# A decode-attention block: eight heads of one batch row at a time, V in 64-KB rows, TensorE in a loop, each engine written by itself

## The chip, the core and the metric

The kernel runs on one core of one Trainium2 chip. The metric is the device time of one execution in microseconds. The kernel before was run three times: the median is 668.3 us, the lowest 667.74 and the highest 669.08.

## What is computed

One decode step of a transformer block for four sequences (B = 4) with one new token each. Everything is bf16 at the boundary.

```python
# x (4,1,640); k_cache, v_cache (4,32,4096,128); wq (640,4096); wo (4096,640); w1 (640,1728); w2 (1728,640)
q = (layernorm(x) @ wq).reshape(4, 1, 32, 128).transpose(0, 2, 1, 3)
p = softmax(einsum("bhqd,bhkd->bhqk", q, k_cache) * 128**-0.5)
o = einsum("bhqk,bhkd->bhqd", p, v_cache)
h = x + o.transpose(0, 2, 1, 3).reshape(4, 1, 4096) @ wo
u = layernorm(h) @ w1 + b1
out = h + (u * tanh(softplus(u))) @ w2
```

The two caches hold 134.2 MB each; wq and wo 5.2 MB each; w1 and w2 2.2 MB each. Every byte of them is read once.

## The kernel before

The attention is done in 32 groups (`NG`). A group is four neighbouring heads of one batch row. Its keys are one tile of 4 MB in SBUF: 128 partitions, 32 of them for each head, and 128 consecutive keys in each partition, which are 32 KB in a row both in memory and in SBUF (L100). The values lie the same way in a second tile. There are two buffers for K tiles and two for V tiles (`KBUFS`, `VBUFS`).

A group's work runs through all engines.

- VectorE multiplies the K tile in place by the query, in four pieces of 4096 elements per partition (L367). The query has been spread over the partitions beforehand (`qbs`).
- TensorE adds each piece up over the 128 columns by multiplying with the identity (L374), eight matmuls of 512 columns to a piece, and VectorE reduces what is left in PSUM to 64 scores per partition (L386), twice to a group.
- The softmax takes the maximum of a partition (L397), brings it to one row by TensorE (L399), takes the maximum of each head (L404), sends it back to the partitions (L412), and ScalarE makes the exponentials (L417), which also writes them spread into the four columns of a head selector `e2`.
- TensorE multiplies V by them (L257, 32 matmuls of 512 columns to a group), ScalarE copies the result out of PSUM (L267), and TensorE adds the blocks up (L273).

The order is written out by hand in one Python loop over the groups, with the framework's schedule switched off; the framework still places the waits and the semaphores. All large loads are issued by SyncE's queue (SP): wq first, then two K tiles and a V tile, and then each next tile as its buffer comes free. The output projection's weights wo come in between groups 8 and 11 in eight loads (L471), and the weights of the MLP, w1 and w2, are the last loads (L502 to L508). Of the last group, K is loaded in two parts and V in four.

At the end stand the last group's softmax, the last projection (L348), the second layernorm, the two MLP products (L564, L629) and a 5-KB store (L653).

Of the kernel before, what the change touches and what calls it, by code (L numbers as in the profile page):

```python
# [12 lines left out]
AX = mybir.AxisListType  # L13


@with_exitstack
def kernel(
# [23 lines left out]

    nc = tc.nc

# [4 lines left out]
    DC = D // 128  # L48
    G = 4
    PH = 128 // G  # L50
    R = Sk // PH
    NP = 2
    RP = R // NP
    W = 512 // RP
    HQ = H // G
    NG = HQ * N
    SCALE = float(Dh) ** -0.5
    EPS = 1e-5
    QC = 512
    WOC = 8  # L60
    NQ = 2
    DQ = Dh // NQ
    VP = 4
    KBUFS = 2
    VBUFS = 2
    NE2 = 2

# [5 lines left out]
    FC = C2 + 1  # L73

    W1_PARTS = ((0, 3), (3, DC))

    ctx.enter_context(tc.manual_schedule())


    pad = ctx.enter_context(tc.tile_pool(name="pad", bufs=1))  # L80
    pad.tile([128, 192], BF16, name="pad")
    kpool = ctx.enter_context(tc.tile_pool(name="kpool", bufs=KBUFS))
    vpool = ctx.enter_context(tc.tile_pool(name="vpool", bufs=VBUFS))
    wbig = ctx.enter_context(tc.tile_pool(name="wbig", bufs=1))
    consts = ctx.enter_context(tc.tile_pool(name="consts", bufs=1))
    work = ctx.enter_context(tc.tile_pool(name="work", bufs=2))

    x_rows = A_x.rearrange("b s d -> (b s) d")
    out_rows = out.rearrange("b s (c p) -> (b s c) p", p=128)


    def load_kv(pool, tag, cache, g, parts):
        hq, b = divmod(g, N)
        t = pool.tile([128, R, Dh], BF16, tag=tag, name=f"{tag}{g}")
        view = cache[b, G * hq : G * (hq + 1)].rearrange("h (p r) d -> (h p) r d", p=PH)

        np_ = parts if g == NG - 1 else 1
        for i in range(np_):
            r0, r1 = i * R // np_, (i + 1) * R // np_
            nc.sync.dma_start(out=t[:, r0:r1, :], in_=view[:, r0:r1, :])  # L100
        return t

    def load_k(g):
        return load_kv(kpool, "kt", A_k_cache, g, NP)

    def load_v(g):
        return load_kv(vpool, "vt", A_v_cache, g, VP)

    x_bf = consts.tile([N, D], BF16)
    nc.scalar.dma_start(out=x_bf[:, :], in_=x_rows[:, :])  # L110

    wq_sb = wbig.tile([128, DC, H * Dh], BF16, tag="w")
    nc.sync.dma_start(out=wq_sb[:, :, :], in_=A_wq.rearrange("(p c) n -> p c n", c=DC))
    kts, vts = {}, {}
    kts[0] = load_k(0)
    kts[1] = load_k(1)
    vts[0] = load_v(0)


    ident = consts.tile([128, 128], BF16)  # L120
    make_identity(nc, ident[:, :])
    ident_f = consts.tile([128, 128], FP32)
    nc.gpsimd.tensor_copy(out=ident_f[:, :], in_=ident[:, :])
    ones_f = consts.tile([128, 128], FP32)
    nc.gpsimd.memset(ones_f[:, :], 1.0)
    mean_f = consts.tile([128, 128], FP32)
    nc.gpsimd.memset(mean_f[:, :], 1.0 / D)
    eps_t = consts.tile([128, 1], FP32)
    nc.vector.memset(eps_t[:, :], EPS)
    nscale = consts.tile([1, 128], FP32)  # L130
    nc.vector.memset(nscale[:, :], -SCALE)
    sel = consts.tile([N, N, G, 128], BF16)
    nc.vector.memset(sel[:, :, :, :], 0.0)
    e2 = [consts.tile([128, R, G], BF16, name=f"e2_{i}") for i in range(NE2)]
    for t in e2:
        nc.gpsimd.memset(t[:, :, :], 0.0)
    rs2 = consts.tile([128, NG, G], FP32)
    nc.gpsimd.memset(rs2[:, :, :], 0.0)
    b1T = consts.tile([128, FC], FP32)
    nc.gpsimd.memset(b1T[:, :], 0.0)  # L140
    otn = consts.tile([128, HQ, N, G], BF16)

    for q in range(G):
        nc.vector.tensor_copy(
            out=sel[:, :, q, q * PH : (q + 1) * PH],
            in_=ident[0:N, 0:N].unsqueeze(2).to_broadcast([N, N, PH]),
        )

    def layernorm_rows(in_sb, out_bf, pool):
        n_sub = 2  # L150
        in_view = in_sb.rearrange("p (n f) -> p n f", n=n_sub)
        stats = pool.tile([N, n_sub, nc.vector.BN_STATS_DIM], FP32, tag="ln_stats")
        for s in range(n_sub):
            nc.vector.bn_stats(out=stats[:, s, :], in_=in_view[:, s, :])
        mv = pool.tile([N, nc.vector.BN_AGGR_DIM], FP32, tag="ln_mv")
        nc.vector.bn_aggr(out=mv[:, :], in_=stats[:, :, :])
        std = pool.tile([N, 1], FP32, tag="ln_std")
        nc.scalar.activation(
            out=std[:, :], in_=mv[:, 1:2], func=ACT.Sqrt, bias=eps_t[0:N, :], scale=1.0
        )  # L160
        rstd = pool.tile([N, 1], FP32, tag="ln_rstd")
        nc.vector.reciprocal(out=rstd[:, :], in_=std[:, :])
        nc.vector.tensor_scalar(
            out=out_bf[:, :],
            in0=in_sb[:, :],
            scalar1=mv[:, 0:1],
            scalar2=rstd[:, :],
            op0=ALU.subtract,
            op1=ALU.mult,
        )  # L170


    ps_cm = tc.tile_pool(name="ps", bufs=1, space=bass.MemoryType.PSUM)
    ps = ps_cm.__enter__()

    ln1_bf = consts.tile([N, D], BF16)
    layernorm_rows(x_bf, ln1_bf, work)
    xT = consts.tile([128, DC, N], BF16)
    xT_res = consts.tile([128, DC, N], FP32)
    ln1_v = ln1_bf[:, :].rearrange("n (p c) -> n c p", c=DC)  # L180
    x_v = x_bf[:, :].rearrange("n (c p) -> n c p", c=DC)
    for src, dst in ((ln1_v, xT), (x_v, xT_res)):
        tp_ps = ps.tile([128, DC, N], FP32, tag="small")
        for c in range(DC):
            nc.tensor.matmul(
                tp_ps[:, c, :], lhsT=src[:, c, :], rhs=ident[0:N, 0:N], start=True, stop=True
            )
        nc.vector.tensor_copy(out=dst[:, :, :], in_=tp_ps[:, :, :])

    q_all = consts.tile([N, H * Dh], BF16)  # L190

    def q_chunk(n):
        q_ps = ps.tile([N, QC], FP32, tag="qq")
        for c in range(DC):
            nc.tensor.matmul(  # L195
                q_ps[:, :],
                lhsT=xT[:, c, :],
                rhs=wq_sb[:, c, n * QC : (n + 1) * QC],
                start=(c == 0),
                stop=(c == DC - 1),  # L200
            )
        nc.scalar.copy(out=q_all[:, n * QC : (n + 1) * QC], in_=q_ps[:, :])  # L202

    def q_broadcast(hq):
        qb_ps = ps.tile([128, N * Dh], FP32, tag="qq")
        for b in range(N):
            for q in range(G):
                h = G * hq + q
                nc.tensor.matmul(  # L209
                    qb_ps[:, b * Dh : (b + 1) * Dh],  # L210
                    lhsT=sel[:, b, q, :],
                    rhs=q_all[:, h * Dh : (h + 1) * Dh],
                    start=(q == 0),
                    stop=(q == G - 1),
                )
        nc.scalar.copy(
            out=qbs[:, hq, :, :], in_=qb_ps[:, :].rearrange("p (b d) -> p b d", d=Dh)
        )

    qbs = consts.tile([128, HQ, N, Dh], BF16)  # L220

    Q_AT = {-1: (0,), **{g: (g + 1,) for g in range(HQ - 1)}}
    WO_AT = {HQ + i: i for i in range(H // WOC)}
    B1_AT = HQ + len(WO_AT) + 1

    PROJ_AT = {B1_AT + 1 + hq: hq for hq in range(4)}
    PROJ_AT.update({4 * (hq + 1) + 2: hq for hq in range(4, HQ - 1)})
    for hq in Q_AT[-1]:
        q_chunk(hq)
        q_broadcast(hq)  # L230

    ot = {}


    J = 4
    T = 4
    p_ps = ps.tile([128, J * Dh], FP32, tag="p")
    nc.vector.memset(p_ps[:, :], 0.0)
    pick = consts.tile([128, J * G], FP32)
    nc.vector.tensor_reduce(  # L240
        out=pick[:, :],
        in_=ident_f[:, :].rearrange("p (t i) -> p i t", t=T)[:, 0 : J * G, :],
        axis=AX.X,
        op=ALU.add,
    )
    blocks = {}

    def ot_of(g):
        hq, b = divmod(g, N)
        if b == 0:  # L250
            ot[hq] = ps.tile([128, N, G], FP32, tag="ot", name=f"ot{hq}")
        return ot[hq][:, b, :]

    def pv_moving(g, r0, r1):
        for r in range(r0, r1, J):
            c0 = 128 // T * (r // J % T)
            nc.tensor.matmul(  # L257
                p_ps[c0 : c0 + J * G, :],
# [6 lines left out]
    def pv_copy(g):  # L265
        blocks[g] = work.tile([128, J * Dh], FP32, tag="p_sb", bufs=1, name=f"p_sb{g}")
        nc.scalar.copy(out=blocks[g][:, :], in_=p_ps[:, :])  # L267
# [159 lines left out]
    for g in range(NG):  # L427
# [28 lines left out]
        if g in PROJ_AT:  # L456
            project(PROJ_AT[g])
# [227 lines left out]
```

## Time and profile before

| | |
|---|---|
| median of three runs | 668.3 us |
| the profiled execution, its own time | 667.85 us |
| its span, first to last instruction | 666.0 us |
| bytes read from HBM | 283.35 MB |
| DMA packets | 13,015 |
| instructions in the trace | 7,152 |
| TensorE busy, mean clock granted | 441.4 us (66%), 0.847 |
| VectorE busy | 353.0 us (53%) |
| ScalarE busy | 115.0 us (17%) |
| wq landed, first K tile landed | 15.95 us, 25.64 us |

The profile shows one execution. Its span leaves out 1.85 us of its own time. An engine's busy time is the time in which it worked on instructions; waits, branches and the issuing of DMAs are not in it. The DMA figures are a mean over the core's 16 DMA engines. The trace also holds a record of every DMA packet, with its start, its length in ns and its bytes.

### The profile page before, as it was taken

Reading aid. Unit: us, or ns where it says so; the run is one execution under the profiler, and the core shown is the slowest. Engines: PE = TensorE matmul, PEld = TensorE weight load, DVE = VectorE, ACT = ScalarE, POOL = GpSimd, SP = SyncE. Lnnn points to the kernel's source line nnn. Section 1 sums busy time; section 2 is a strip of 40 time slices with the busy share of each in tenths; the row PEclk is TensorE's granted clock in tenths of the full one; section 3 lists DMA queues with packets and bytes.
Section 4 is the critical chain, followed back from the end, with each engine's and each line's share of the span. In section 5 each row is a group of like instructions: output and inputs, shape, how many; then the busy total and the mean of one; then the engine's idle time right before and its main releaser. Section 6 shows DMA issues by size and latency. Waiting matters only on the chain.

```text
span 666.0 us, 7152 instructions
## 1 busy us (share of the span) xinstructions
PE 441.4 (66%) x3105; PEld 203.4 (31%) x3105; DVE 353.0 (53%) x308; ACT 115.0 (17%) x352; POOL 2.4 (0%) x13
## 2 busy tenths in 40 slices
PE   0588777886666475367666857766557785667786
PEld 0233333343223232133222323322223232223345
DVE  2486454466645266246654545657444666455742
ACT  0022122131101111011111111111011111011131
POOL 1000000000000000000000000000000000000000
PEclk9997799797778977797777798778788797788985
DMA  9999999999999999999999999999999999999996
GB/s 376 439 434 421 436 440 428 426 434 441 428 427 434 431 428 428 435 433 430 435 437 424 431 437 438 421 434 441 434 418 437 440 433 422 436 437 434 423 419 266
DMA packets 13015, 283.81 MB, mean 426 GB/s; under 512 B 1395, under 2 KB 2103, under 8 KB 4152
## 3 DMA queue, kind: packets, MB, share of 16 engines
q1 hardware_dynamic: 12976, 283.36, 99.0%
q8 instruction: 24, 0.39, 0.2%
q14 instruction: 7, 0.06, 0.0%
q10 hardware_dynamic: 8, 0.01, 0.0%
HBM read 283.35 MB, written 0.01 MB: 425 GB/s over the span
## 4 chain that ended last, share of the span: by engine, by line
DMA 67%; DVE 17%; PE 15%; issue 1%; SPq 0%; DVEq 0%
DMA kt<-in_A_k_cache_dram 62%; DVE kt L367 14%; PE s L374 13%; DMA vt<-in_A_v_cache_dram 3%; DMA w<-in_B_w_dram 2%; DVE s_sb L386 2%; PE tr L399 1%; PE ot L273 1%; SPq L506 0%; DVE mx L404 0%; PE p_ps L257 0%; DVE pm L397 0%; PE o L332 0%; PE tr L412 0%; PE y2T L629 0%
## 5 line engine op out<-in xcount | busy, mean ns | idle before, releaser
L374 PE MATMUL s<-kt,ident 128*128 128x512 bf16 x1024 | 297.0, 443 | 194.3 <-DVE kt L367 191.9
L367 DVE TENSOR_TENSOR kt<-kt,qbs 128x4096 bf16<-128x4096 bf16 x128 | 291.5, 2279 | 239.4 <-DMA kt<-in_A_k_cache_dram 239.4
L374 PEld LDWEIGHTS <-ident 128*128 128x128 bf16 x1024 | 109.6, 110 | 339.8 <-issue 169.5
L417 ACT ACTIVATE e<-s_sb,nbs 32x128 bf16<-32x128 f32 x128 | 74.0, 578 | 2.5
L414 ACT COPY nbs<-tr 128x4 f32<-128x4 f32 x32 | 5.2, 162 | 330.8 <-PE tr L412 330.8
L257 PE MATMUL p_ps<-vt,e 128*16 128x512 bf16 x1008 | 62.2, 390 | 0.0
L386 DVE TENSOR_REDUCE s_sb<-s 128x64 f32<-128x512 f32 x64 | 43.5, 680 | 3.9 <-PE s L374 3.9
L267 ACT COPY p_sb<-p_ps 128x512 f32<-128x512 f32 x32 | 18.8, 586 | 151.0 <-PE p_ps L257 151.0
L273 PEld LDWEIGHTS ot<-pick,p_sb 128*128 128x128 f32 x256 | 33.7, 193 | 5.8 <-ACT p_sb L267 1.5
L257 PEld LDWEIGHTS <-e 128*16 128x16 bf16 x1008 | 22.7, 90 | 37.4 <-issue 16.6
L417 ACT ACTIVATION_READ_ACCUMULATOR e<-s_sb,nbs 32x1 f32 x128 | 32.2, 252 | 0.0
L273 PE MATMUL ot<-pick,p_sb 128*128 128x4 f32 x256 | 30.9, 244 | 0.9 <-ACT p_sb L267 0.7
L404 DVE TENSOR_REDUCE mx<-tr 1x4 f32<-1x128 f32 x32 | 8.9, 277 | 24.3 <-PE tr L399 24.3
L195 PE MATMUL q_ps<-wq_sb,xT 128*4 128x512 bf16 x40 | 11.0, 409 | 9.6 <-DMA wq_sb<-in_A_wq_dram 9.6
L399 PE MATMUL tr<-ident_f,pm 128*1 128x128 f32 x64 | 15.6, 337 | 1.2 <-DVE pm L397 1.2
L412 PEld LDWEIGHTS tr<-mx,nscale 1*128 1x128 f32 x64 | 9.3, 182 | 13.8 <-issue 11.9
L304 DVE RECIPROCAL rl<-l_ps 128x16 f32<-128x16 f32 x8 | 2.1, 258 | 20.9 <-PE l_ps L296 20.9
L209 PE MATMUL qb_ps<-q_all,sel 4*128 4x128 bf16 x128 | 9.2, 225 | 5.3 <-ACT q_all L202 5.3
L412 PE MATMUL tr<-mx,nscale 1*128 1x4 f32 x64 | 12.2, 258 | 0.4 <-DVE mx L404 0.4
L209 PEld LDWEIGHTS <-sel 4*128 4x128 bf16 x128 | 8.4, 98 | 9.1 <-issue 9.1
L202 ACT CAST q_all<-q_ps 4x512 bf16<-4x512 f32 x8 | 4.6, 575 | 34.5 <-PE q_ps L195 34.5
L399 PEld LDWEIGHTS tr<-ident_f,pm 128*1 128x1 f32 x64 | 2.8, 81 | 23.4 <-issue 23.4
(85 smaller groups left out, 78.0 us busy)
## 6 DMA issues: line engine op xcount, KB each, us to landing
kt<-in_A_k_cache_dram SPq DMA_DIRECT2D x31, 4096.0 KB, 25.2
vt<-in_A_v_cache_dram SPq DMA_DIRECT2D x31, 4096.0 KB, 33.1
wq_sb<-in_A_wq_dram SPq DMA_DIRECT2D x1, 5120.0 KB
wo_sb<-in_A_wo_dram SPq DMA_DIRECT2D x8, 640.0 KB, 37.4
kt<-in_A_k_cache_dram SPq DMA_DIRECT2D x2, 2048.0 KB
vt<-in_A_v_cache_dram SPq DMA_DIRECT2D x4, 1024.0 KB, 20.0
w<-in_B_w_dram SPq DMA_DIRECT2D x1, 1296.0 KB
w<-in_B_w_dram SPq DMA_DIRECT2D x2, 640.0 KB, 18.2
```

Source lines behind the costliest of these rows:

```text
L195: nc.tensor.matmul(q_ps[:, :], lhsT=xT[:, c, :], rhs=wq_sb[:, c, n * QC : (n + 1) * QC], start=(c == 0), stop=(c == DC - 1),)
L209: nc.tensor.matmul(qb_ps[:, b * Dh : (b + 1) * Dh], lhsT=sel[:, b, q, :], rhs=q_all[:, h * Dh : (h + 1) * Dh], start=(q == 0), stop=(q == ...
L257: nc.tensor.matmul(p_ps[c0 : c0 + J * G, :], lhsT=e2[g % NE2][:, r : r + J, :].rearrange("p j q -> p (j q)"), rhs=vts[g][:, r : r + J, :]. ...
L267: nc.scalar.copy(out=blocks[g][:, :], in_=p_ps[:, :])
L273: nc.tensor.matmul(o, lhsT=p_sb[:, j * Dh : (j + 1) * Dh], rhs=pick[:, j * G : (j + 1) * G], start=(j == 0), stop=(stop and j == J - 1),)
L367: nc.vector.tensor_tensor(out=kt[:, :, d0 : d0 + DQ], in0=kt[:, :, d0 : d0 + DQ], in1=qbs[:, hq, b, d0 : d0 + DQ].unsqueeze(1).to_broadcas ...
L374: nc.tensor.matmul(s_ps[:, :, :], lhsT=ident[:, :], rhs=kt[:, :, d : d + W], start=(d == 0), stop=(d == Dh - W),)
L386: nc.vector.tensor_reduce(out=s_sbs[g][:, part * RP : (part + 1) * RP], in_=s_of.pop((g, part))[:, :, :], axis=AX.X, op=ALU.add,)
L399: nc.tensor.matmul(tr_ps[0:1, 0:128], lhsT=pm[:, :], rhs=ident_f[:, :], start=True, stop=True)
L404: nc.vector.tensor_reduce(out=mx[:, :], in_=tr_ps[0:1, 0:128].rearrange("o (a b) -> o a b", a=G), axis=AX.X, op=ALU.max,)
L412: nc.tensor.matmul(nb_ps, lhsT=nscale[:, :], rhs=mx[:, :], start=True, stop=True)
L417: nc.scalar.activation(out=e2[g % NE2][p0:p1, :, q], in_=s_sb[p0:p1, :], func=ACT.Exp, bias=nb[p0:p1, q : q + 1], scale=SCALE, accum_out=r ...
```

## The change

The kernel is written anew for the attention; the MLP's operations at the end stay as they were.

- The framework's waits are gone. Each engine's instructions are written one engine after the other, and all waits are on a few semaphores of the kernel's own.
- The unit is an octet: eight heads of one batch row, 16 octets in all. A partition holds 256 keys of a head, 64 KB. K is loaded in two halves of 4 MB (`kt[0]`, `kt[1]`), 32 KB to a partition, one buffer for each half. V is one load of 8 MB, 64 KB to a partition, with one buffer.
- The last two octets, U and L, are two batch rows of four heads each: octet U holds heads 24 to 27, and L heads 28 to 31, of batch rows 2 and 3. Their loads come in pairs of 64 rows, one for the even and one for the odd partitions.
- TensorE's work for the first 14 octets is a loop on the engine (`Fori`), with its body written once. The identity is loaded as weights once to an octet (`mm_held`) rather than once to each matmul. SyncE, VectorE and ScalarE have their 14 octets written out.
- The queries of all heads are made at the start, in one accumulation of 40 matmuls. The selector for eight heads is made on VectorE from 256 exponentials to a partition (`e1`, `e`).
- The waits for buffers: the next octet's K halves wait until TensorE has read the present ones; the next V waits until TensorE has multiplied the present one. At the end SyncE waits for `pv_a` and `pv_b`, the two halves of octet U's product with V, before it loads the two halves of octet L's V.

The main parts of the new text:

```python
    def pe_pieces():                      # TensorE: 8 pieces of 8 matmuls
        te.ldweights(ident[:, :])
        ...
    def pe_softmax():                     # TensorE: three short matmuls, and a wait for the selector
        ...
    def dve_scores(u, done):              # VectorE: 8 multiplications, 4 reductions
        ...
    def softmax(u, done, e):
        to_pe.by(ve.tensor_reduce(out=pm[:, :], in_=s_sb[:, :], axis=AX.X, op=ALU.max))
        after(ve, done[0])
        ...
        to_pe.by(ve.tensor_reduce(out=o, in_=i, axis=AX.X, op=ALU.max))
        after(ve, done[1])
        then(ve, dve, ve.tensor_tensor(out=nb8[:, :], in0=nb_ps, in1=m[:, :], op=ALU.mult))
        after(ac, dve.by(ve.tensor_reduce(out=nbs[:, :], in_=nb8[:, :], axis=AX.X, op=ALU.add)))
        exp_ok = act.by(ac.activation(out=e1[:, :], in_=s_sb[:, :], func=ACT.Exp, ..., accum_out=rs[:, u : u + 1]))
        after(ve, exp_ok)
        to_pe.by(ve.tensor_tensor(out=rs8[:, :], ...))
        to_pe.by(ve.tensor_tensor(out=e, in0=e1[:, :].unsqueeze(2).to_broadcast([128, R, R8]),
                                  in1=m[:, :].unsqueeze(1).to_broadcast([128, R, R8]), op=ALU.mult))
        ...
    # SyncE, octets 0 to 13
    load_k(0); load_k(1); load_v(0)
    for u in range(NL):
        for k in range(KT):
            after(sp, loop_event(u, (k + 1) * NP * NQ - 1))   # TensorE has read this half
            load_k(KT * (u + 1) + k)
        after(sp, loop_event(u, PV))                          # TensorE has multiplied V
        if u < NL - 1:
            load_v(u + 1)
        ...                                                   # wo, b1 in octets 4 to 7
    # VectorE and ScalarE, octets 0 to 13
    for u in range(NL):
        dve_scores(u, ...)
        after(ve, softmax(u, ..., e2[0]))
        act_copy(loop_event(u, PV))
        otn_ok = normalise(u, loop_event(u, OT))
    # TensorE, octets 0 to 13
    with nc.Fori(0, NL, engines=[PE], head_slot={PE: 0}):
        pe_pieces()
        pe_softmax()
        take(v_in, 16)
        pe.by(pv_moving(e2[0], 0, R, R))
        pe.by(add_blocks(ot_ps[0]))
    # the last two octets, U = 14 and L = 15
    load_v(NL, 0, RK)
    ...
    done_u = pe_pieces()
    after(sp, done_u[NP * NQ - 1]);  load_k(KT * L)
    after(sp, done_u[-1]);           load_k(KT * L + 1, NP);  load_v(U, RK, R)
    dve_scores(U, done_u);  done_s = pe_softmax();  softmax(U, done_s, e2[0])
    after(te, v_ready[U, 0])
    pv_a = pe.by(pv_moving(e2[0], 0, RK, R))
    after(sp, pv_a);                 load_v(L, 0, RK)
    done_l = pe_pieces()
    dve_scores(L, done_l);  done_s = pe_softmax();  after(ve, softmax(L, done_s, e2[1]))
    after(te, v_ready[U, RK])
    pv_b = pe.by(pv_moving(e2[0], RK, R, R))
    after(sp, pv_b)
    V_LAST = (RK, R - R // 4, R - R // 8, R)
    for r0, r1 in zip(V_LAST, V_LAST[1:]):
        load_v(L, r0, r1)
    ...                                   # then w1 and w2, and the MLP as before
```

## The prediction

> **What bounds the kernel now.** I read the page's slices and DMA part first.
>
> ```profile
> PE   0588777886666475367666857766557785667786
> DVE  2486454466645266246654545657444666455742
> DMA  9999999999999999999999999999999999999996
> DMA packets 13015, 283.81 MB, mean 426 GB/s; under 512 B 1395, under 2 KB 2103, under 8 KB 4152
> q1 hardware_dynamic: 12976, 283.36, 99.0%
> q8 instruction: 24, 0.39, 0.2%
> ```
>
> The DMA engines are full in every slice but the last; TensorE and VectorE never are. The packet records give the price: a 32-KB packet took 1213 ns (median of 7,936, and the same at the 1st and 99th percentiles), a 16-KB one 611, a 40-KB one 1514. That is 9 ns to a packet and 0.602 us to each 16 KB. Adding up all packets and dividing by 16 engines gives 661.2 us of the 666.0 us span. So the time is the sum of the packets, plus a start, plus a tail; an engine matters only where it lets the queue run dry.
>
> Whether it can, SyncE's waits and the issues show.
>
> ```profile
> SPq L100 <- DVE kt L367: 470.2, 30, 33.4
> kt<-in_A_k_cache_dram SPq DMA_DIRECT2D x31, 4096.0 KB, 25.2
> vt<-in_A_v_cache_dram SPq DMA_DIRECT2D x31, 4096.0 KB, 33.1
> ```
>
> A 4-MB load needs 8 packets on each engine, 9.7 us; from issue to landing it took 25.2 us (K) and 33.1 (V). So each waited 15 us or more behind others: the queue is that deep, and SyncE's own long waits cost nothing.
>
> Last the two ends, in the timeline and the windows.
>
> ```profile
> 25.69 6.70 DVE L367 TENSOR_TENSOR kt<-kt,qbs 128x4096 bf16<-128x4096 bf16 x3 [18.32 <-DMA kt<-in_A_k_cache_dram]
> 642.33 3.14 PE L257 MATMUL p_ps<-vt,e 128*16 128x512 bf16 x32
> 656.00:662.00 6.00, 3.96 (x110) 3.86 (x107) 1.96 (x9) 2.00 (x4) 0.00 (x0) 0.50 0.70 277
> 662.00:666.00 4.00, 1.22 (x21) 0.85 (x21) 0.50 (x2) 0.00 (x0) 0.00 (x0) 0.50 0.01 2
> 663.91 0.33 SPq L653 DMA_DIRECT2D out_dram<-out_bf  x1
> ```
>
> The last weights land at 662; 4 us of tail follow, which the change leaves alone. At 656 to 662 the DMA share is 0.70: the 16 engines run out up to 2 us apart, mainly because 24 packets of 16 KB with instructions fell on them unevenly.
>
> **V in 64-KB rows.** 14 octets load V by 128 rows of 64 KB instead of 256 of 32 KB: 112 packets fewer per engine, 9 ns each: -1.0 us. If the rows are cut into two packets on the way, 0. I take -1.0, since 40 KB went as one packet.
>
> **TensorE in a loop.** The program holds some 920 TensorE instructions instead of 5,650, so most of the 24 instruction packets go, if the loop's body isn't fetched anew each time. A packet costs one engine 0.6 us. The mean engine has 0.9 us of them, and the slowest ends 1.6 us after the mean (packet records), so the end moves by 0 (all refetched) to -1.9. I take -1.0, the middle. TensorE itself has slack: 30 us of work in 39.
>
> **The start.** All queries now come before any score: 40 matmuls from 16.0 (some 10 at 0.43 us cold, the rest 0.23), a copy of 0.57 and five of 0.6 put the first multiplication at 31.5 instead of 25.7. The first half is then free at 42; wq, two K halves and 8 MB of V keep the queue until 53. Cost 0; with that cover gone it would be 6 us.
>
> **The octets.** With K0 landing at t, K1 lands at t+9.7 and V at t+29. VectorE needs 8 multiplications of 2.24 us and four reductions of 0.68: the halves are free at t+11 and t+22, needed at t+29 and t+39. V is multiplied by t+35, needed at t+48. VectorE waits in order for that product (`normalise`) and is back before t+38.7, when the next K0 lands. Margins of 13 to 18 us: cost 0, V's single buffer too. Weights held rather than reloaded, fewer ScalarE instructions and the selector on VectorE lie under the same cover.
>
> **The last octet.** Here the cover ends. `pv_b` gates the last 4 MB of V, and w1 and w2 stand behind it on SP; TensorE does it only after octet L's whole softmax. From the landing T of L's first K half, the queue still holds L's second half and two V halves: 3 x 9.7 = 29.1 us, less 1.3 because a landing is seen that long after its last packet. It is dry at T+27.9. The chain to the next packet:
>
> - 8 multiplications (6.70/3 each) and three reductions: 19.9
> - the last piece on TensorE: 1.9
> - last reduction to exponential: 2.5 in the old tail (640.11 to 642.63), 2.8 with twice the scores and two more short operations
> - exponential with its sum: 0.7 (0.6 now for half the width); the row-sum product 0.2
> - selector, 2048 results: 1.1 at the multiplication's 0.56 ns each, 2.2 at the reduction's rate of about 1.05 ns. I take 2.2, because one input repeats a number eight times and no fast row does that
> - 32 matmuls with V: 3.1 as at 642.33, after 2 us of idle TensorE; 1.9 in steady work. I take 3.1, because TensorE has just idled 6 us
> - semaphore hops 0.3; issue to first packet 0.8 (store at 663.91, packet at 664.7)
>
> Sum T+32.0, so the queue stands empty 4.1 us; bounds 1.6 (short selector, warm matmuls, no hops) and 5.
>
> The 64-row loads of U and L carry the same bytes in the same 32-KB packets: cost 0. The nearest row is the 64-partition load of w2's rest, whose 1280-byte packets took 55 ns like those of 128 partitions. [...]
>
> **Sum.** 666.0 - 1.0 - 1.0 + 4.1 = 668.1 us of span. The profiled execution adds 1.85 and lies 0.45 under the median, so the median becomes 668.1 + 2.3 = 670.4 us.
>
> **Rivals.**
>
> - *The gap never opens (faster).* If the last softmax's chain is under some 28.5 us, the packets' gain stands alone: 666.0 - 2.0 + 2.3 = 666.3. For it: the chain's last three terms are each bounded well below what I took. Against it: even the lower ends leave 1.6 us; it decides for faster only below 0.7.
> - *64-KB rows go as two packets*: the change doesn't do what it says, +1.0: 671.4.
> - *The 64-row loads clash* and their packets take twice as long: U and L are 8 x 9.7 us, +78, and the gap vanishes in it: 744. For it: nothing in the traces. Against: the w2 row.
> - *The new row pitch slows HBM.* K is now read at 32 KB out of every 64, V in 64-KB rows. If packets took 1% longer, 620 us become 626: 676.6. Against: 40-KB rows of wq and 32-KB rows cost the same per byte. [...]
>
> **Chances.** Forecast 0.66: with the gap between 1.6 and 5 and the fetch term between 0 and -1.9 it gives slower 0.41, same 0.24, faster 0.01. No gap 0.17 (faster 0.15, same 0.02). Two packets 0.07 (slower 0.05, same 0.02). Clash 0.05 and pitch 0.05, both slower. Together faster 0.16, same 0.28, slower 0.56; the line is 0.2%, 1.3 us, about what a measurement of this kernel can tell from no change. The range of 666.4 to 674.5 takes in the forecast's bounds, two packets and most of the no-gap case; it leaves out the clash, most of the pitch and the edge below, 0.2 in all.
>
> **What would show it.** V packets of 64 KB at 2417 ns and 32-KB ones still at 1213; fewer than 24 instruction packets; K0 of the last octet landing near 610; a hole in the DMA share of 3 to 5 us at 638 to 643, ended by `pv_b`; the last weights at 664. It is wrong if the DMA share stays at 1.00 through there, if any packet of octets 14 and 15 is longer than its size says, or if the queue runs dry in the first octets.

## The result, and the profile after

The changed kernel takes 675.06 us (median of five, 673.69 to 676.75), the kernel before 668.3 (five runs) beside it: a ratio of 1.0105 with a 95% interval of 1.0085 to 1.0124. It is slower, as forecast, but by 6.8 us where 2.1 were forecast, and 0.56 us above the range. The profiled execution took 674.94 us.

The page of the changed kernel: the slices of TensorE and DMA, the GB/s, and the DMA part.

```profile
span 673.1 us, 5296 instructions
PE   0785767576575655746656466656748665776656
DMA  9999999999999999999999999999999999999966
GB/s 372 436 439 430 443 421 448 415 458 432 409 463 407 461 401 432 440 430 450 421 446 438 411 442 426 442 423 428 454 411 458 411 462 411 434 415 394 415 249 268
DMA packets 11011, 283.50 MB, mean 421 GB/s; under 512 B 1331, under 2 KB 2039, under 8 KB 4088
q1 hardware_dynamic: 10992, 283.36, 98.1%
q8 instruction: 6, 0.10, 0.1%
```

2,000 packets are gone, and instruction packets fell from 24 to 6. Up to slice 38 the DMA share is as before; the last two slices, 33.7 us, move 249 and 268 GB/s. The span is 7.1 us longer. The windows show where the queue is not full (us; busy time and count on PE, PEld, DVE, ACT, POOL; then granted clock, DMA share, GB/s):

```profile
606.00:610.00 4.00, 1.24 (x7) 0.41 (x4) 1.72 (x5) 0.53 (x2) 0.00 (x0) 1.00 0.86 315
636.00:640.00 4.00, 1.53 (x6) 1.08 (x6) 1.97 (x6) 0.60 (x2) 0.00 (x0) 0.66 0.68 295
640.00:646.00 6.00, 3.87 (x38) 1.90 (x38) 1.32 (x2) 0.59 (x1) 0.00 (x0) 0.66 0.07 14
646.00:650.00 4.00, 3.04 (x72) 1.97 (x71) 0.17 (x1) 0.17 (x1) 0.00 (x0) 1.00 0.97 373
656.00:660.00 4.00, 3.74 (x82) 3.66 (x83) 0.17 (x1) 1.29 (x2) 0.00 (x0) 0.50 1.01 411
664.00:668.00 4.00, 2.00 (x61) 1.90 (x60) 1.78 (x8) 1.26 (x3) 0.00 (x0) 0.50 0.86 320
```

From about 639 to 646 nothing is loaded, where a hole of 4.1 us was forecast; by the packet records the 16 engines lose 6.65 us there. A smaller dent, which was not forecast, lies at 606 to 610. The timeline of the changed kernel shows the chain around both (start, length, engine, line, out<-in, count, and in brackets the idle time before and what ended it):

```profile
580.54 3.02 PE L199 MATMUL yT_b<-o,w_sb 128*128 128x4 bf16 x107
586.14 0.51 PE L199 MATMUL yT_b<-o,w_sb 128*128 128x4 bf16 x13 [2.59 <-issue]
586.51 6.80 PE L203 MATMUL s<-kt,ident 128*128 128x512 bf16 x24
612.39 0.20 DVE L563 RECIPROCAL rl<-small 128x8 f32<-128x8 f32 x1
612.51 6.64 DVE L508 TENSOR_TENSOR kt<-kt,qbs 128x4096 bf16<-128x4096 bf16 x3
638.20 0.51 ACT L535 ACTIVATE e<-s_sb,nbs 128x256 bf16<-128x256 f32 x1 [28.13 <-DVE nbs L533]
638.92 2.28 DVE L555 TENSOR_TENSOR kt<-e,mask 128x2048 bf16<-128x2048 bf16 x1
641.35 3.25 PE L199 MATMUL p_ps<-v_sb,e 128*32 128x512 bf16 x32 [1.63 <-PEq L196]
644.64 3.71 SPq L266 DMA_DIRECT2D v_sb<-in_A_v_cache_dram  x6
653.25 1.90 PE L199 MATMUL p_ps<-v_sb,kt 128*32 128x512 bf16 x16 [3.90 <-DMA v_sb<-in_A_v_cache_dram]
655.93 1.85 PE L199 MATMUL ot_b<-pick,p_sb 128*128 128x8 f32 x8 [0.78 <-PEq L196]
```

The order is the forecast one: octet L's softmax, its selector (L555), then `pv_b` (641.35), then the issue of the last V (644.64). But VectorE starts octet L at 612.51. The first three lines say why: TensorE reaches octet U's pieces only at 586.51, behind the 120 matmuls of the output projection for heads 0 to 23, with a pause of 2.59 us among them. An instruction packet of 881 ns starts in that pause, at 583.6; with the loop written out (experiment 4) the 120 stand in one row of 3.36 us. That the pause comes from leaving the loop was not tested. L563 (612.39) is the last operation of octet U's softmax on VectorE. After 653.25 no instruction of the profile's last chain waits for a DMA: TensorE, at a clock of 0.50, with short steps on VectorE and ScalarE, runs on to the end.

### The profile page after: what moved, and what is told of

The parts are those of the page before. It is cut to its first block, busy times and chain, and to the rows that moved or that the text cites. A ratio compares the mean times of both kernels' runs of the same rounds, so it can differ in the third digit from the quotient of the medians.

```text
span 673.1 us, 5296 instructions
## 1 busy us (share of the span) xinstructions
PE 422.3 (63%) x2727; PEld 85.9 (13%) x1719; DVE 390.6 (58%) x362; ACT 28.4 (4%) x65; POOL 0.8 (0%) x7
## 5 line engine op out<-in xcount | busy, mean ns | idle before, releaser
L203 PE MATMUL s<-kt,ident 128*128 128x512 bf16 x1024 | 267.4, 414 | 125.4 <-PEq L196 125.4
L199 PE MATMUL p_ps<-v_sb,e 128*32 128x512 bf16 x960 | 89.0, 550 | 31.8 <-PEq L196 31.8
L199 PEld LDWEIGHTS p_ps<-v_sb,e 128*32 128x32 bf16 x960 | 36.6, 131 | 77.3 <-issue 72.4
L555 DVE TENSOR_TENSOR e<-e,mask 128x2048 bf16<-128x2048 bf16 x15 | 34.3, 2284 | 0.0
L535 ACT ACTIVATE e<-s_sb,nbs 128x256 bf16<-128x256 f32 x16 | 8.1, 507 | 465.1 <-DVE nbs L533 465.1
L199 PE MATMUL ot_b<-pick,p_sb 128*128 128x8 f32 x128 | 17.3, 262 | 12.5 <-PEq L196 12.5
L199 PE MATMUL small<-rs,ones_f 128*128 128x8 f32 x32 | 7.2, 297 | 22.1 <-PEq L196 22.1
L199 PEld LDWEIGHTS ot_b<-pick,p_sb 128*128 128x128 f32 x128 | 16.3, 199 | 20.4 <-issue 20.4
L199 PE MATMUL h_b<-w_sb,xz 128*32 128x512 bf16 x40 | 10.3, 425 | 11.3 <-DMA w_sb<-in_A_wq_dram 11.3
L567 ACT COPY p_sb<-p_ps 128x512 f32<-128x512 f32 x16 | 9.4, 586 | 134.6 <-PE p_ps L199 134.6
## 6 DMA issues: line engine op xcount, KB each, us to landing
v_sb<-in_A_v_cache_dram SPq DMA_DIRECT2D x6, 2048.0 KB, 20.5
```

The lines of the kernel that those rows point to most:

```text
L199: return te.matmul(out_, lhsT=lhsT, rhs=rhs, start=start, stop=stop)
L203: return te.add_instruction(mybir.InstMatmult(name=nc.get_next_instruction_name(), engine=PE, ins=[te.lower_ap(rhs), te.lower_ap(lhsT, for ...
L535: ac.activation(out=e1[:, :], in_=s_sb[:, :], func=ACT.Exp, bias=nbs[:, :], scale=SCALE, accum_out=rs[:, u : u + 1],)
L555: ve.tensor_tensor(out=e, in0=e1[:, :].unsqueeze(2).to_broadcast([128, R, R8]), in1=m[:, :].unsqueeze(1).to_broadcast([128, R, R8]), op=AL ...
L567: p_out.by(ac.copy(out=p_sb[:, :], in_=p_ps[:, :]))
```

## The experiments

Every ratio is to the kernel before on the same chip (medians 667.8 to 667.9 there).

**1. `pv_b` ahead of octet L's softmax.** Is the gate the cause?

```diff
-    done_s = pe_softmax()
-    after(ve, softmax(L, done_s, e2[1]))
     after(te, v_ready[U, RK])
     pv_b = pe.by(pv_moving(e2[0], RK, R, R))
+    done_s = pe_softmax()
+    after(ve, softmax(L, done_s, e2[1]))
```

> The one edit: octet U's second V product (pv_b) is put on TensorE before octet L's softmax instead of behind it. Theory A (the stream's hole before the last V loads is the loss): pv_b ends near 637 us instead of 644.6, the last V loads are issued before the queue runs dry at 639.5, the hole of 6.6 us and the 0.65 us of slow first packets go, and the median falls from 675.1 to 668.0 +- 1. Theory B (the 64-row loads or the new row pitch are slow in themselves): the hole closes but the time stays above 672. Theory C (TensorE's loop stalls the stream): no change, 675.

669.71 us, 1.0028 (1.0018 to 1.0038): about 5 us come back by moving 32 matmuls (5.35 by the medians, 5.1 by the ratios). That is 0.7 us above the 667 to 669 that were expected. The timeline and the windows of this kernel:

```profile
636.18 1.91 PE L199 MATMUL p_ps<-v_sb,e 128*32 128x512 bf16 x32
638.14 4.20 SPq L266 DMA_DIRECT2D v_sb<-in_A_v_cache_dram  x6
597.00:600.00 3.00, 2.57 (x12) 0.00 (x0) 3.00 (x3) 0.00 (x0) 0.00 (x0) 1.00 0.84 284
606.00:610.00 4.00, 2.21 (x12) 0.28 (x4) 1.39 (x3) 0.00 (x0) 0.00 (x0) 1.00 0.85 348
638.00:646.00 8.00, 4.17 (x34) 2.94 (x33) 3.26 (x7) 1.07 (x3) 0.00 (x0) 0.75 0.93 369
```

V is issued 6.5 us earlier and the hole is closed; the product takes 1.91 us where TensorE comes to it straight out of its pieces, and 3.25 in the changed kernel, behind 1.63 us of idle time. Two dents are there, at 597 and 606; the first is not in the profiled execution of the changed kernel. The gate is shown as the main cause; the rest stays above the kernel before.

**2. The output projection of heads 0 to 23 later**, behind the first half of octet L's V, so that octet U starts earlier. The gate stays.

```diff
-    after(te, o4_ok, wo_in)
-    for hq in range(QA): project(hq)
     ...                                   # octets U and L, first half of L's V multiplied
+    after(te, o4_all, wo_in)              # o4_all = o4_ok
+    for hq in range(QA): project(hq)
```

> The one edit: the projections of heads 0 to 23, which TensorE does between the loop and octet U, go to the end, behind the first half of octet L's V product. Theory A: octet U's first pieces start 3.5 us earlier, its second K half is free before the queue thins out at 608, so the half-dry spell there (0.45 us idle and 1.7 us of slow packets) goes, and octet L's chain starts about 1 us earlier, so the hole is about 5.5 us: 672 +- 1. Theory B: the slow 16-KB packets near 610 stay, 675.

674.56 us (four runs, 672.1 to 676.21), 1.0106 (1.0091 to 1.0121). The profiled execution, 672.1, meets the expectation; the median misses it, and against the changed kernel's 675.06 no gain is shown. In this execution the dent is gone (by the packet records no engine idles there), VectorE has to wait 1.17 us for octet L's keys, and `pv_b` starts 3.0 us earlier. The hole is 5.6 us by the packet records, as expected (5.5):

```profile
606.00:610.00 4.00, 0.98 (x8) 0.67 (x10) 2.82 (x5) 0.60 (x2) 0.00 (x0) 0.61 0.93 397
610.75 6.70 DVE L508 TENSOR_TENSOR kt<-kt,qbs 128x4096 bf16<-128x4096 bf16 x3 [1.17 <-DMA kt<-in_A_k_cache_dram]
638.37 3.20 PE L199 MATMUL p_ps<-v_sb,e 128*32 128x512 bf16 x32 [1.84 <-PEq L196]
641.61 3.74 SPq L266 DMA_DIRECT2D v_sb<-in_A_v_cache_dram  x6
```

**3. Both moves, those of 1 and 2.**

> Both edits at once. Theory A: no hole and no half-dry spell, the packets' sum (660.7 us less 1.7 of slow packets) plus start and tail: 666.0 +- 1, faster than the kernel before by the 1.0 us of fewer V packets and 0.9 of fewer instruction packets. Theory B: 672 or more.

670.8 us, 1.0045 (1.0032 to 1.0058): 4.8 us over what was expected. There is no hole and no dent, and the last packet ends at 660.8. But this kernel's timeline has the projection ahead of the last V's products:

```profile
644.15 3.16 PE L199 MATMUL yT_b<-o,w_sb 128*128 128x4 bf16 x120
653.67 1.85 PE L199 MATMUL ot_b<-kt,v_sb 128*128 128x8 bf16 x64
666.24 0.33 SPq L180 DMA_DIRECT2D out_dram<-out_bf  x1
```

With the queue early, TensorE's chain is the end: the work that was moved off octet U's path now lies on the last one.

**4. The loop written out 14 times** (`for _ in range(NL):` in place of `nc.Fori`). Does TensorE's loop cost anything?

> TensorE's 14 octets written out instead of a loop, all else as changed. Theory A: 18 more instruction packets of 0.6 us on single engines, 0.7 us for the mean engine; the hole at the end lets the engines meet again, so most unevenness is lost: 675.8 +- 0.8. Theory C (the loop's branch or the fetch of its body stalls TensorE): 670 or less.

674.69 us, 1.0108 (1.0093 to 1.0123), with 18 instruction packets, 12 more than with the loop and not the 18 more that were expected: the same as with the loop, within what this measures, and just below the expected 675.0 to 676.6. The loop doesn't cause the loss; its gain isn't seen either while the gate sets the end.

```profile
583.01 3.36 PE L199 MATMUL yT_b<-o,w_sb 128*128 128x4 bf16 x120
q8 instruction: 18, 0.29, 0.2%
```

**5. `pv_b` early, and the projection in octet L's softmax**, where TensorE waits for VectorE: 60 of its matmuls behind the second short matmul and 60 behind the third.

```diff
     ...                                   # pv_b ahead, as in 1; the old projection loop is gone
+    after(te, o4_all, wo_in)
+    done_s = pe_softmax([lambda: [project(hq) for hq in range(0, QA // 2)],
+                         lambda: [project(hq) for hq in range(QA // 2, QA)]])
```

> pv_b ahead of octet L's softmax, as in the first experiment, and the 120 projection matmuls of heads 0 to 23 in that softmax's idle time on TensorE, half of them behind its second and half behind its third short matmul. Theory A (only TensorE's order in the last two octets costs): no hole, no half-dry spell at 598 and 609, and unlike the experiment that did both edits no 3.2 us of projections ahead of the last V product: data end near 660.8, span 665 and median 666.8 +- 1, a little faster than the kernel before. Theory B (the 64-row loads or the new row pitch are slow): 670 as before.

666.25 us, 0.9978 (0.9968 to 0.9989): faster than the kernel before, and within what was expected. Eight of its twelve executions took 666.1 to 666.5 and four 667.8 to 668.5, the profiled one (668.24) among the four; what tells them apart stays open. Its timeline and a window:

```profile
583.08 8.14 PE L203 MATMUL s<-kt,ident 128*128 128x512 bf16 x24 [2.91 <-PEq L196]
633.55 1.91 PE L199 MATMUL p_ps<-v_sb,e 128*32 128x512 bf16 x32
635.50 4.06 SPq L266 DMA_DIRECT2D v_sb<-in_A_v_cache_dram  x6
636.41 1.66 PE L199 MATMUL yT_b<-o,w_sb 128*128 128x4 bf16 x60
638.16 1.64 PE L199 MATMUL yT_b<-o,w_sb 128*128 128x4 bf16 x60
638.00:646.00 8.00, 7.29 (x121) 4.96 (x118) 2.20 (x3) 0.17 (x1) 0.00 (x0) 0.62 1.00 418
663.67 0.33 SPq L180 DMA_DIRECT2D out_dram<-out_bf  x1
```

The 120 matmuls fit into waits that TensorE had anyway, octet U starts at 583.08, and the DMA share is 1.00 where the hole was. Against experiment 1, which has the projection in its old place, this is 0.5% faster by the ratios.

**6. The same with V of octets 0 to 13 in two loads of 32-KB rows**: the price of the packets alone, now that no hole covers it.

```diff
-            load_v(u + 1)
+            load_v(u + 1, 0, RK)
+            load_v(u + 1, RK, R)
     ...                                   # the first V and TensorE's wait likewise
```

> The kernel e5_mid, with V of octets 0 to 13 in two loads of 32-KB rows each instead of one of 64-KB rows. By the packet price, 112 packets of 9 ns more on each engine: +1.0 us over e5_mid. By the rival that the row pitch slows HBM, no change, since the pitch stays 64 KB and the packets are as before.

666.89 us, 0.9991 (0.9981 to 1.0001), 0.64 over experiment 5 (1.0 was expected); the two intervals overlap, but its lower seven executions (666.68 to 666.91) all lie above the lower eight of experiment 5. The packet records agree: all packets added up and divided by 16 rise by 1.3 us, of which V's own packets make 0.9, with the 7,936 packets of 32 KB at 1213 ns again.

**7. Experiment 5 with the loop written out.**

> The kernel e5_mid with TensorE's 14 octets written out instead of the loop. 18 instead of 6 instruction packets: +0.5 us if they fall evenly, up to +1.9 if one engine gets most of them, since no hole lets the engines meet again. If the loop stalls TensorE: faster than e5_mid by 1 us or more.

668.58 us, 1.0011 (1.0001 to 1.0022), 2.3 over experiment 5 and the intervals apart: a little more than expected. It has 18 instruction packets where experiment 5 has 6. The last chain of its profile waits for V until 652.28, when the last DMA engine lands its part; the others have landed theirs by 651.05. In experiment 5 the last part of V has landed by 649.44, and that chain waits for no DMA. The two profiled executions are only 0.5 us apart, so they don't show the whole 2.3.

**8. Experiment 5 with each K half of octets 0 to 13 in two loads, partitions 0 to 63 and 64 to 127**: what do 64 partitions in a row cost?

```diff
-            yield slice(0, 128), view.rearrange("h (p r) d -> (h p) r d", p=PH)[:, k0:k1, :]
+            rows_ = view.rearrange("h (p r) d -> (h p) r d", p=PH)
+            if cache is A_k_cache:
+                yield slice(0, 64), rows_[0:64, k0:k1, :]
+                yield slice(64, 128), rows_[64:128, k0:k1, :]
+            else:
+                ...                       # V as before
```

> The kernel e5_mid, with each K half of octets 0 to 13 as two loads of 64 rows, one for partitions 0 to 63 and one for 64 to 127. If 64 partitions in a row take the full rate, as the packets of w2's rest seemed to say: no change, 667. [...]

One execution: 988.11 us, 320 over experiment 5's profiled one; packets twice as long in the 28 halves would have given 272 (28 x 8 x 1.213). Windows of this kernel, in the octets with such loads and in the last two, whose loads keep to even and odd partitions:

```profile
400.00:460.00 60.00, 25.97 (x142) 4.04 (x79) 22.02 (x20) 1.19 (x3) 0.00 (x0) 0.73 1.00 292
880.00:920.00 40.00, 26.59 (x180) 5.19 (x109) 24.92 (x24) 1.42 (x4) 0.00 (x0) 0.83 0.92 392
```

The DMA share is 1.00 and 0.92, but the rate is 292 and 392 GB/s: the 32-KB packets of the first kind took 2504 ns in the mean (median 2559), those of octets 14 and 15 1213 (median). That is 2.1 times as long, and 28 halves of 8 packets make 289 us of it (28 x 8 x 1.291). Another 27 us are V's 64-KB packets, which took 2661 ns in the mean here and not 2418, for a cause that was not tested.

**9. The changed kernel with w1's two loads ahead of the last V**, so that the queue has something to carry in the hole. If the idle queue costs the time, some of it comes back; if the lateness of V does, none.

```diff
+    after(sp, done_l[NP * NQ - 1])
+    for c0, c1 in W1_PARTS: load(f"w1_{c0}", ...)
     after(sp, pv_b)
     ...                                   # the last loads of V
```

> The changed kernel with the two loads of w1 (2.2 MB, 5.3 us of packets) issued ahead of the last V loads instead of behind them, all waits as they were. If what costs is that the queue stands empty, 5.3 of the 6.6 us of hole are filled and the median falls to 670 +- 1. If what costs is that the last V loads wait for pv_b and the whole end of the kernel hangs on them, the hole is filled but these loads still land at the same time: the data end moves from 668.7 to about 663.5 us of the span, the end by no more than the last matmuls' wait for w2, and the median stays at 674.5 +- 1.

675.98 us, 1.0113 (1.0094 to 1.0132), 0.5 above the upper end expected for a late V. The hole shrinks to some 2.3 us and the last packet ends at 666.0 instead of 668.7 (663.5 was expected), but the end doesn't move forward:

```profile
645.77 3.98 SPq L266 DMA_DIRECT2D v_sb<-in_A_v_cache_dram  x6
654.49 1.90 PE L199 MATMUL p_ps<-v_sb,kt 128*32 128x512 bf16 x16 [4.00 <-DMA v_sb<-in_A_v_cache_dram]
```

So it is the late V. Its first part has landed 8.6 us after the issue in the changed kernel and 8.7 here, and some 20 us of TensorE's chain follow. From the issue of the last V to the end of the span, kernels that keep the gate all take the same time, whatever else they move:

| kernel | last V issued | span | difference |
|---|---|---|---|
| after | 644.64 | 673.1 | 28.5 |
| 2, projection later | 641.61 | 670.3 | 28.7 |
| 4, loop written out | 644.02 | 672.8 | 28.8 |
| 9, w1 first | 645.77 | 674.2 | 28.5 |
| 1, `pv_b` early | 638.14 | 667.3 | 29.2 |
| 5, both in place | 635.50 | 666.4 | 30.9 |

In the last two V comes early enough to queue behind other loads, so issue and end part.

## Why the prediction was right in sign and too small

**The failed step is the +4.1 of the last octet.** Its mechanism is right (experiment 1), its size is not. The prediction's own chain has VectorE start at T near 610, the last V issued at T+31.2 and the span end 26.9 later, at 668.1. (Its terms as printed add up to T+31.9; it has T+32.0.) Against the trace:

- *Start: 612.5, not 610: +2.5.* T was taken as the landing of the keys. By the landing records they were complete at 610.6, which is 0.6 of it. For the other 1.9 VectorE was still in octet U's softmax (612.39), because the projection and the pause in it held TensorE until 586.5. The prediction looked only at what the chain waits for in octet L, and gave the projection, which stands between the loop and octet U, no place. With it elsewhere, VectorE waits for the keys and starts at 610.75 (experiment 2), and octet U's first product with V starts 2.1 us earlier (610.54 in experiment 5, 612.62 after). This is read from single traces: in the medians, experiment 2 shows no gain, and only without the gate does the projection's place show in the time (experiment 5 against 1).
- *Chain: 32.1, not 31.2: +0.9.* Each term was near: multiplications and reductions 20.5 to the end of the last one (19.9), reduction to exponential 3.15 (2.8), selector 2.28 (2.2), 32 matmuls with V, behind 1.63 us of idle time, 3.25 (3.1; straight out of the pieces they took 1.91 in experiment 1).
- *From issue to end: 28.5, not 26.9: +1.6.* The first packet came 1.3 us after the issue (0.8 was taken from the last store), and the first packets of the refilled queue lost another 0.6 us an engine (the first of each engine took 1138 ns in the mean, where 16 KB otherwise take 611). The rest is that not the last weights but TensorE's chain behind the last V is the end (experiment 9), which the prediction did not cost.

2.5 + 0.9 + 1.6 is 5.0, and 673.1 - 668.1 is 5.0. The queue ran dry at about 639.5 (mean of the engines) and not at 637.9. That the dent at 606 to 610 did this fits experiment 2, which has no dent and runs dry at 637.5. So the hole was 6.65 us and not the 8.0 that 4.1 + 2.5 + 0.9 + 0.5 would give. The prediction's 1.3 us between last packet and landing is no delay of that length: of octet L's first half of V the mean engine ends at 639.5, the last packet at 640.70, and the landing is complete at 641.07.

**The bounds 1.6 to 5 were too narrow for the same reason.** They varied the lengths of the terms and held the start fixed. The start and the end behind the issue missed by more than any of those terms.

**Right:** V packets of 64 KB took 2418 ns (1,792 of them), so "two packets" is refuted, and experiment 6 finds 0.9 us in V's packets for the -1.0. 32-KB packets stayed at 1213 ns, so reading K at 32 KB out of every 64 cost nothing here; the 1% of that rival was the author's assumption. The start cost nothing: the first multiplication came at 29.93 (31.5 forecast) with the queue full (DMA share 1.03 from 16 to 30 us, 1.01 from 30 to 54). The first 14 octets cost nothing (from 30 to 583 us a DMA share of 1.00 and 433 GB/s).

**Right in sign, invisible in the result and mis-sized:** the -1.0 for the loop. Between 34.3 and 583.6 us the changed kernel has no 16-KB instruction packet, so no new fetch of the loop's body shows. Experiment 4 finds nothing of the gain; experiment 7 finds 2.3 us, over the upper bound of 1.9. The price of 0.6 us a packet was that of a 16-KB load: the 24 instruction packets of the kernel before took 0.94 us each, which is 1.4 us for the mean engine and not 0.9.

**Right by a poor argument:** the 64-row loads of octets 14 and 15 cost nothing. The w2 row that was set against a clash was no evidence, as experiment 8 shows: in loads of 64 partitions in a row a 32-KB packet took 2504 ns in the mean and not 1213, while the 1280-byte packets of w2's 64 partitions had taken 55 ns like those of 128. That a clash doubles the time was the author's assumption before the runs; the 2504 ns are 2.1 times as much. The split into even and odd partitions, which the kernel has, kept the 1213 ns.

**Not sharp enough:** the hole's end on `pv_b` and its place were forecast; the last weights came at 668.7, not 664.

## What to carry to other kernels

Where a late load is gated by a product, the time is that load's issue plus everything behind it (28.5 to 28.8 us in the four kernels above that keep the gate): cost the gate from the first engine that is late, one stage further back than the wait itself, and look there for work that a rewrite has put in front. An engine's work that only has to be done some time belongs into that engine's own waits, not between two stages of the critical chain (experiments 3 and 5 differ in nothing else, by some 4.5 us). A saving on a full queue shows only once nothing else sets the end (the loop: none with the hole, 675.06 us against 674.69, and 2.3 without it, 666.25 against 668.58), so measure it with the hole closed.

## What the runs showed of the hardware that was not expected

- Two loads to partitions 0 to 63 and 64 to 127 took 2504 ns in the mean for a 32-KB packet, two loads to even and odd partitions 1213 ns, the same as one load to all 128.
- The DMA queue that had run dry restarted slowly: 1.3 us from issue to first packet, and the run's 16-KB packets took 687 ns in the mean against a median of 611, most of the long ones being those behind the hole and the dent.
- With the loop written out, 12 more instruction packets of 16 KB went with 2.3 us more on a full queue, though their own time over 16 engines is 0.7 us (12 x 0.94 / 16). One engine landed its part of V over 1 us after the others, and the last chain waited for it; that this is the whole of the difference was not tested.
